# A quarter of the output projection's weights loaded early by GpSimd into partitions 64 to 127, in transfers of 8 rows

## The chip, the cores and the metric

One core of one Trainium2 chip. The metric is the time of one execution in device microseconds (us). The kernel before takes 192.46 us (median of 4 runs, 192.37 to 192.64).

## The reference

Grouped-query attention over a cache, with one projection before it and one after it; everything is bf16.

```python
q = (x @ wq).reshape(B, Sq, Hq, Dh).transpose(0, 2, 1, 3)        # B 8, Sq 4, D 512, Hq 32, Dh 128
k = jnp.repeat(k_cache, 4, axis=1); v = jnp.repeat(v_cache, 4, axis=1)   # 8 KV heads, Sk 2048
p = softmax(einsum("bhqd,bhkd->bhqk", q, k) * Dh ** -0.5)
o = einsum("bhqk,bhkd->bhqd", p, v)
out = o.transpose(0, 2, 1, 3).reshape(B, Sq, Hq * Dh) @ wo         # wo: 4096 x 512
```

The caches are 64 MB, wq and wo 4 MB each. All of it must be read once.

## The kernel before

The work is cut into 32 units (a pair of KV heads and a batch row). A unit loads 1 MB of K and 1 MB of V, each a 128-partition transfer of 8 KB rows, all from the Sync engine's queue, as buffers come free. TensorE (PE) transposes K, forms the scores, then the values and the sums of the softmax, in 64 half-unit steps. wo has four quarters of 1 MB. The parts that the change touches:

```python
loads = []
for u in range(NU + KA):                      # NU = 32, KA = 4
    if u < NU:
        loads.append(("k", u))
    if u >= KA - 1 and u - KA + 1 < NU:
        loads.append(("v", u - KA + 1))
    if u in (NU, NU + 1):                     # wo between the last three V
        loads.append(("wo", (u - NU, 0, WR if u == NU else 4)))
# ...
def to_wo_rows(p):                            # the heads' output, transposed to wo's row order
    perm = psum_l.tile([128, WR, T], BF16, tag="l", name="perm")
    for r in range(WR):                       # WR = 8
        nc.tensor.transpose(perm[:, r, :],
            nats[p][:, :, :].rearrange("t q r -> t r q")[:, r, :], ident[:T, :T])
    nc.vector.tensor_copy(out=oP[p][:, :, :], in_=perm[:, :, :])

def project(p, r0, n):                        # one quarter: 8 row groups x 2 column halves
    for half in range(2):
        for r in range(r0, r0 + n):
            nc.tensor.matmul(out_ps[half][:, :], lhsT=oP[p][:, r, :],
                rhs=wo_sb[:, p, r, half * DH : (half + 1) * DH],
                start=(p == 0 and r == 0), stop=(p == G2 - 1 and r == WR - 1))
# ...
        if step == NH - 1 - 2 * VB:           # all K and V issued: the rest of wo
            load_wo(1, 4, 4); load_wo(2, 0, WR); load_wo(3, 0, 4); load_wo(3, 4, 2); load_wo(3, 6, 2)
        if step == NH - 5:
            # out_ps allocated
            project(0, 0, WR)
        elif step == NH - 3:
            project(1, 0, 4)
# then: to_tokens(3), project(1, 4, 4), to_wo_rows(3), project(2, ..), project(3, ..), output
```

The softmax here doesn't subtract the row's maximum and nothing guards it: scores larger than these inputs give would overflow.

Of the kernel before, what the change touches and what calls it, by code (L numbers as in the profile page):

```python
# [8 lines left out]
BF16 = mybir.dt.bfloat16  # L9
# [5 lines left out]
def kernel(  # L15
# [9 lines left out]
    nc = tc.nc  # L25

    B, Sq, D = x.shape
# [4 lines left out]
    T = B * Sq  # L32
    R = D // 128
    G2 = Hkv // 2
# [3 lines left out]
    HP = 2 * rep  # L38
    scale = float(Dh) ** -0.5
    NU = G2 * B  # L40
    NH = 2 * NU
    KB = 7
    VB = 6
    L = 6
    KA = L // 2 + 1
    WR = HP
    DH = D // 2
# [5 lines left out]
    const = ctx.enter_context(tc.tile_pool(name="const", bufs=1))  # L53
    wpool = ctx.enter_context(tc.tile_pool(name="wpool", bufs=1))
    kpool = ctx.enter_context(tc.tile_pool(name="kpool", bufs=KB))
    vpool = ctx.enter_context(tc.tile_pool(name="vpool", bufs=VB))
# [5 lines left out]
    psum_l = ctx.enter_context(tc.tile_pool(name="psum_l", bufs=1, space=bass.MemoryType.PSUM))  # L62
# [12 lines left out]
    ident4 = const.tile([128, 128], FP32, name="ident4")  # L75
    oT_all = const.tile([128, Hq, B, Sq], BF16, name="oT_all")
    out_sb = [const.tile([T, DH], BF16, name=f"out_sb{i}") for i in range(2)]
    oP = [const.tile([128, WR, T], BF16, name=f"oP{p}") for p in range(G2)]
    ident = const.tile([128, 128], BF16, name="ident")
    ones = const.tile([128, 128], BF16, name="ones")  # L80
    probs = [const.tile([128, C, NQ], BF16, name=f"probs{i}") for i in range(L // 2 + 2)]
# [25 lines left out]
    def load_wo(p, r0, n):  # L107
        rows = wo[p * HP * 128 : (p + 1) * HP * 128, :].rearrange("(q r) j -> q r j", r=WR)
        nc.sync.dma_start(wo_sb[:, p, r0 : r0 + n, :], rows[:, r0 : r0 + n, :])
# [3 lines left out]
    loads = []  # L113
    for u in range(NU + KA):
        if u < NU:
            loads.append(("k", u))
        if u >= KA - 1 and u - KA + 1 < NU:
            loads.append(("v", u - KA + 1))
        if u in (NU, NU + 1):
            loads.append(("wo", (u - NU, 0, WR if u == NU else 4)))  # L120
    loads.reverse()

    def load_ready(nk, nv):

        while loads:
            kind, u = loads[-1]
            if kind == "wo":
                loads.pop()
                load_wo(*u)
                continue  # L130
            if u >= (nk + KB if kind == "k" else nv + VB):
                return
# [7 lines left out]
    for e in range(2):  # L140
        for g in range(2):
            nc.vector.tensor_copy(
                out=pick[:, e, g, :], in_=ident[:, :].rearrange("d (k e) -> d e k", e=2)[:, e, :]
# [12 lines left out]
    for p in range(G2):  # L156
        psq = psum_s.tile([128, HP, T], FP32, tag="s", name="psq")
        for h in range(HP):
            hh = p * HP + h
            for r in range(R):  # L160
                nc.tensor.matmul(  # L161
                    psq[:, h, :],
                    lhsT=wq_sb[:, r, hh * 128 : (hh + 1) * 128],
                    rhs=xT_sb[:, r, :],
                    start=(r == 0),
# [3 lines left out]
            out=qT_all[:, p, :, :, :],  # L169
            in_=psq[:, :, :].rearrange("d h (b s) -> d b h s", b=B),  # L170
            mul=scale,
        )
    for p in range(G2):
        pse = psum_s.tile([128, 2, B, NQ], FP32, tag="s", name="pse")
        for e in range(2):
            nc.tensor.matmul(  # L176
                pse[:, e, :, :],
                lhsT=pick[:, e, :, :],
                rhs=qT_all[:, p, :, :, :].rearrange("d b h s -> d (b h s)"),
                start=True,  # L180
                stop=True,
            )
        for g in range(2):
            rows = slice(g * 64, (g + 1) * 64)
            (nc.scalar.copy if g else nc.vector.tensor_copy)(  # L185
                out=q_bd[rows, p, :, :, g, :], in_=pse[rows, :, :, :]
            )

    wo_sb = wpool.tile([128, G2, WR, D], BF16, tag="w", name="wo_sb")
    kt = {}  # L190

    def transpose_part(i, part):
        u, hf = divmod(i, 2)
        c0 = hf * HC + part * (HC // 2)
        kp = psum_k.tile([128, HC // 4, 128], FP32, tag="k", name="kp")
        k4 = ks[u][:, :, :].rearrange("s c d -> s (c d)").bitcast(FP32)
        for j in range(HC // 4):
            w = (c0 // 2 + j) * 128
            nc.tensor.transpose(kp[:, j, :], k4[:, w : w + 128], ident4[:, :])  # L199
        kp2 = kp[:, :, :].rearrange("k j s -> k (j s)").bitcast(BF16)  # L200
        k_t = ktpool.tile([128, HC // 4, 128, 2], BF16, tag="kt", name="kt")
        kt2 = k_t[:, :, :, :].rearrange("k j s e -> k (j s e)")
        if part == 1 and hf == 1:
            nc.scalar.copy(out=kt2, in_=kp2)  # L204
        else:
            nc.vector.tensor_copy(out=kt2, in_=kp2)  # L206
        kt[(i, part)] = k_t

    def scores(i):
        u, hf = divmod(i, 2)  # L210
        p, b = units[u]
        pr = probs[u % len(probs)]
        s_ps = psum_s.tile([128, HC, NQ], FP32, tag="s", name="s_ps")
        for j in range(HC // 2):
            k_t = kt[(i, j // (HC // 4))]
            for e in range(2):
                nc.tensor.matmul(  # L217
                    s_ps[:, 2 * j : 2 * j + 2, :],
                    lhsT=k_t[:, j % (HC // 4), :, e],
                    rhs=q_bd[:, p, e, b, :, :],  # L220
                    start=(e == 0),
                    stop=(e == 1),
                )
        for g in range(2):
            rows = slice(g * 64, (g + 1) * 64)
            cols = slice(g * NQ // 2, (g + 1) * NQ // 2)
            nc.scalar.activation(  # L227
                out=pr[rows, hf * HC : (hf + 1) * HC, cols], in_=s_ps[rows, :, cols], func=EXP
            )
# [3 lines left out]
    def values(i):  # L233
        u, hf = divmod(i, 2)
        p, b = units[u]
        pr = probs[u % len(probs)]
        if hf == 0:
            o_ps[u] = psum_o.tile([128, NQ], FP32, tag="o", name="o_ps")
        for c in range(HC):
            cc = hf * HC + c  # L240
            nc.tensor.matmul(  # L241
                o_ps[u][:, :],
                lhsT=vs[u][:, cc, :],
                rhs=pr[:, cc, :],
                start=(cc == 0),
                stop=(cc == C - 1),
            )
# [3 lines left out]
    def norms(u):  # L251
        pr = probs[u % len(probs)]
        l_ps = psum_l.tile([128, LC, NQ], FP32, tag="l", name="l_ps")
        for c in range(0, C, LC):
            nc.tensor.matmul(  # L255
                l_ps[:, :, :],
                lhsT=ones[:, :],
                rhs=pr[:, c : c + LC, :],
                start=(c == 0),
                stop=(c + LC == C),  # L260
            )
        l_sb = small.tile([128, NQ], FP32, tag="l_sb", name="l_sb")
        nc.vector.tensor_reduce(  # L263
            out=l_sb[:, :], in_=l_ps[:, :, :].rearrange("d c q -> d q c"), axis=AX, op=ADD
        )
        r_sb = small.tile([128, NQ], FP32, tag="r_sb", name="r_sb")
        nc.vector.reciprocal(r_sb[:, :], l_sb[:, :])  # L267
        r_sbs[u] = r_sb
# [10 lines left out]
    nats = {}  # L279
# [14 lines left out]
        nats[p] = nat_sb  # L294

    def to_wo_rows(p):
        perm = psum_l.tile([128, WR, T], BF16, tag="l", name="perm")
        for r in range(WR):
            nc.tensor.transpose(
                perm[:, r, :],  # L300
                nats[p][:, :, :].rearrange("t q r -> t r q")[:, r, :],
                ident[:T, :T],
            )
        nc.vector.tensor_copy(out=oP[p][:, :, :], in_=perm[:, :, :])

    def project(p, r0, n):
        for half in range(2):
            for r in range(r0, r0 + n):
                nc.tensor.matmul(  # L309
                    out_ps[half][:, :],  # L310
                    lhsT=oP[p][:, r, :],
                    rhs=wo_sb[:, p, r, half * DH : (half + 1) * DH],
                    start=(p == 0 and r == 0),
                    stop=(p == G2 - 1 and r == WR - 1),
                )

    for step in range(-L - 1, NH):
        i, j = step + L + 1, step + L
        if i < NH:
            transpose_part(i, 0)  # L320
        if 0 <= j < NH:
            scores(j)
        if i < NH:
            transpose_part(i, 1)
        u, hf = divmod(step, 2)
        if step >= 0:
            p, b = units[u]
            if hf == 0:
                norms(u)
            values(step)  # L330
            if hf == 1:
                finish(u)
            elif p > 0 and b == 1:
                to_tokens(p - 1)
            elif p > 0 and b == 2:
                to_wo_rows(p - 1)
        load_ready(min((i + 1) // 2, NU), max((step + 1) // 2, 0))
        if step == NH - 1 - 2 * VB:
            assert not loads
            load_wo(1, 4, 4)  # L340
            load_wo(2, 0, WR)
            load_wo(3, 0, 4)
            load_wo(3, 4, 2)
            load_wo(3, 6, 2)
        if step == NH - 5:
            out_ps = [
                psum_s.tile([T, DH], FP32, tag="s", name=f"out_ps{n}") for n in range(2)
            ]
            project(0, 0, WR)
        elif step == NH - 3:  # L350
            project(1, 0, 4)

    to_tokens(3)
    project(1, 4, 4)
    to_wo_rows(3)
    project(2, 0, WR)
    project(3, 0, 4)
    project(3, 4, 2)
    project(3, 6, 2)
# [35 lines left out]
```

## Time and profile before

| what | before | where it is read |
|---|---|---|
| time | 192.46 us | median of the runs |
| span of the profiled execution | 191.0 us | page |
| DMA engines' time, main queue | 95.5% of the span | page, queues |
| PE busy | 81% | page |
| last K landed | 166.35 us | chain of waits |
| PE waits for data after that | 2.75 us | PE timeline |

A queue's share is the time of its packets over 16 engines' span.

### The profile page before, as it was taken

Reading aid. Unit: us, or ns where it says so; the run is one execution under the profiler, and the core shown is the slowest. Engines: PE = TensorE matmul, PEld = TensorE weight load, DVE = VectorE, ACT = ScalarE, POOL = GpSimd, SP = SyncE. Lnnn points to the kernel's source line nnn. Section 1 sums busy time; section 2 is a strip of 40 time slices with the busy share of each in tenths; the row PEclk is TensorE's granted clock in tenths of the full one; section 3 lists DMA queues with packets and bytes.
Section 4 is the critical chain, followed back from the end, with each engine's and each line's share of the span. In section 5 each row is a group of like instructions: output and inputs, shape, how many; then the busy total and the mean of one; then the engine's idle time right before and its main releaser. Section 6 shows DMA issues by size and latency. Waiting matters only on the chain.

```text
span 191.0 us, 6460 instructions
## 1 busy us (share of the span) xinstructions
PE 154.4 (81%) x2892; PEld 139.7 (73%) x2892; DVE 113.9 (60%) x220; ACT 86.2 (45%) x170; POOL 1.1 (1%) x8
## 2 busy tenths in 40 slices
PE   0019887899999999988888888988886899997783
PEld 0008776799999998877778888877775788885572
DVE  6401754577776777666666667766664677662420
ACT  2003466656566654555555444454554455551000
POOL 2000000000000000000000000000000000000000
PEclk9999999999999999999999999999999999999999
DMA  6999999999999999999999999999999999999940
GB/s 220 439 412 422 419 420 422 420 413 429 410 419 419 417 420 419 417 425 415 420 420 419 422 415 420 419 419 420 415 419 424 415 422 419 415 419 419 399 184 8
DMA packets 10539, 75.97 MB, mean 398 GB/s; under 512 B 1200, under 2 KB 1296, under 8 KB 1936
## 3 DMA queue, kind: packets, MB, share of 16 engines
q1 hardware_dynamic: 10464, 75.55, 95.5%
q8 instruction: 22, 0.36, 0.8%
q14 instruction: 5, 0.04, 0.1%
q10 hardware_dynamic: 48, 0.02, 0.0%
HBM read 75.53 MB, written 0.03 MB: 396 GB/s over the span
## 4 chain that ended last, share of the span: by engine, by line
DMA 90%; PE 7%; ACT 0%; DVE 0%; issue 0%; SPq 0%
DMA k_sb<-in_k_cache_dram 74%; DMA wo_sb<-in_wo_dram 9%; DMA x_sb<-in_x_dram 6%; PE psq L161 2%; PE out_ps L309 2%; PE kp L199 2%; PE pse L176 1%; DVE q_bd L185 0%; PE s_ps L217 0%; ACT q_bd L185 0%; PE xtp L152 0%; SPq L111 0%; ACT out_sb L362 0%; DVE xT_sb L155 0%
## 5 line engine op out<-in xcount | busy, mean ns | idle before, releaser
L199 PE MATMUL kp<-ident,k_sb 128*128 128x128 f32 x512 | 80.9, 284 | 10.6 <-DMA k_sb<-in_k_cache_dram 10.4
L206 DVE COPY kt<-kp 128x1024 bf16<-128x1024 bf16 x96 | 65.5, 685 | 26.6 <-PE kp L199 25.9
L227 ACT ACTIVATE probs<-s_ps 64x256 bf16<-64x256 f32 x128 | 48.3, 378 | 68.7 <-PE s_ps L217 67.9
L199 PEld LDWEIGHTS kp<-ident,k_sb 128*128 128x128 f32 x512 | 55.2, 143 | 12.0 <-issue 11.4
L217 PE MATMUL s_ps<-q_bd,kt 128*128 128x64 bf16 x1024 | 42.3, 193 | 3.1 <-ACT kt L204 2.6
L217 PEld LDWEIGHTS <-kt 128*128 128x128 bf16 x1024 | 39.7, 98 | 4.8 <-ACT kt L204 3.1
L241 PEld LDWEIGHTS <-v_sb 128*128 128x128 bf16 x1024 | 34.3, 96 | 9.4 <-DMA v_sb<-in_v_cache_dram 2.0
L263 DVE TENSOR_REDUCE l_sb<-l_ps 128x32 f32<-128x512 f32 x32 | 22.1, 692 | 24.5 <-PE l_ps L255 24.5
L241 PE MATMUL o_ps<-probs,v_sb 128*128 128x32 bf16 x1024 | 35.0, 176 | 1.0 <-DMA v_sb<-in_v_cache_dram 0.9
L204 ACT COPY kt<-kp 128x1024 bf16<-128x1024 bf16 x32 | 32.4, 1012 | 0.8
L255 PE MATMUL l_ps<-probs,ones 128*128 128x512 bf16 x64 | 19.1, 379 | 0.0
L267 DVE RECIPROCAL r_sb<-l_sb 128x32 f32<-128x32 f32 x32 | 11.3, 353 | 1.1
L152 PE MATMUL xtp<-ident,x_sb 32*128 32x32 bf16 x4 | 0.5, 189 | 13.7 <-DMA x_sb<-in_x_dram 13.5
L152 PEld LDWEIGHTS <-x_sb 32*128 32x128 bf16 x4 | 0.3, 112 | 13.8 <-DMA x_sb<-in_x_dram 13.5
L309 PE MATMUL out_ps<-wo_sb,oP 128*32 128x256 bf16 x64 | 7.6, 272 | 1.7 <-DMA wo_sb<-in_wo_dram 1.7
L168 ACT ACTIVATE qT_all<-psq 128x256 bf16<-128x256 f32 x4 | 1.5, 383 | 14.8 <-PE psq L161 14.8
L309 PEld LDWEIGHTS <-oP 128*32 128x32 bf16 x64 | 6.1, 96 | 2.5 <-issue 1.7
L362 ACT CAST out_sb<-out_ps 32x256 bf16<-32x256 f32 x1 | 0.4, 361 | 15.6 <-PE out_ps L309 15.6
L272 DVE TENSOR_TENSOR oT_all<-o_ps,r_sb 128x32 bf16<-128x32 f32 x32 | 5.8, 182 | 1.7 <-PE o_ps L241 1.5
L255 PEld LDWEIGHTS <-ones 128*128 128x128 bf16 x64 | 6.0, 98 | 0.8 <-issue 0.4
L185 DVE CAST q_bd<-pse 64x512 bf16<-64x512 f32 x4 | 2.6, 683 | 4.7 <-PE pse L176 4.7
L155 DVE COPY xT_sb<-xtp 128x32 bf16<-128x32 bf16 x4 | 0.5, 170 | 7.0 <-PE xtp L152 7.0
(23 smaller groups left out, 34.4 us busy)
## 6 DMA issues: line engine op xcount, KB each, us to landing
k_sb<-in_k_cache_dram SPq DMA_DIRECT2D x32, 1024.0 KB, 20.3
v_sb<-in_v_cache_dram SPq DMA_DIRECT2D x32, 1024.0 KB, 20.2
wq_sb<-in_wq_dram SPq DMA_DIRECT2D x1, 4096.0 KB, 12.5
wo_sb<-in_wo_dram SPq DMA_DIRECT2D x2, 1024.0 KB, 19.2
wo_sb<-in_wo_dram SPq DMA_DIRECT2D x3, 512.0 KB, 18.0
wo_sb<-in_wo_dram SPq DMA_DIRECT2D x2, 256.0 KB, 13.6
x_sb<-in_x_dram SPq DMA_DIRECT2D x1, 32.0 KB, 12.3
out_dram<-out_sb SPq DMA_DIRECT2D x1, 16.0 KB, 1.4
```

Source lines behind the costliest of these rows:

```text
L161: nc.tensor.matmul(psq[:, h, :], lhsT=wq_sb[:, r, hh * 128 : (hh + 1) * 128], rhs=xT_sb[:, r, :], start=(r == 0), stop=(r == R - 1),)
L199: nc.tensor.transpose(kp[:, j, :], k4[:, w : w + 128], ident4[:, :])
L204: nc.scalar.copy(out=kt2, in_=kp2)
L206: nc.vector.tensor_copy(out=kt2, in_=kp2)
L217: nc.tensor.matmul(s_ps[:, 2 * j : 2 * j + 2, :], lhsT=k_t[:, j % (HC // 4), :, e], rhs=q_bd[:, p, e, b, :, :], start=(e == 0), stop=(e == 1),
L227: nc.scalar.activation(out=pr[rows, hf * HC : (hf + 1) * HC, cols], in_=s_ps[rows, :, cols], func=EXP)
L241: nc.tensor.matmul(o_ps[u][:, :], lhsT=vs[u][:, cc, :], rhs=pr[:, cc, :], start=(cc == 0), stop=(cc == C - 1),)
L255: nc.tensor.matmul(l_ps[:, :, :], lhsT=ones[:, :], rhs=pr[:, c : c + LC, :], start=(c == 0), stop=(c + LC == C),)
L263: nc.vector.tensor_reduce(out=l_sb[:, :], in_=l_ps[:, :, :].rearrange("d c q -> d q c"), axis=AX, op=ADD)
L267: nc.vector.reciprocal(r_sb[:, :], l_sb[:, :])
L272: nc.vector.tensor_tensor(out=oT_all[:, p * HP : (p + 1) * HP, b, :], in0=o_ps[u][:, :].rearrange("d (h s) -> d h s", h=HP), in1=r_sbs[u][ ...
L309: nc.tensor.matmul(out_ps[half][:, :], lhsT=oP[p][:, r, :], rhs=wo_sb[:, p, r, half * DH : (half + 1) * DH], start=(p == 0 and r == 0), st ...
```

## The change

The intent, as the code shows it: one quarter of wo no longer comes through the queue that bounds the kernel. GpSimd loads it at the start into a tile of its own, in partitions 64 to 127, as eight transfers of 8 partitions, four apart. Each has a 4 KB transfer ahead of it that nobody reads. The quarter then has 64 partitions with 16 row groups in place of 128 with 8, so PE does 16 transposes and 32 matmuls for it, in place of 8 and 16.

```diff
+    HI = 2
-        if u in (NU, NU + 1):
-            loads.append(("wo", (u - NU, 0, WR if u == NU else 4)))
+        if u == NU:
+            loads.append(("wo", (0, 0, 4)))
+    wo_hi = const.tile([128, 2 * WR, D], BF16, name="wo_hi")
+    spare = const.tile([8, DH], BF16, name="spare")
+    wo2 = wo[2 * HP * 128 : 3 * HP * 128, :].rearrange("(q r) j -> q r j", r=2 * WR)
+    for base in (0, 32):
+        for m in range(4):
+            lo = base + m
+            nc.gpsimd.dma_start(spare[:, :], x.flatten_outer_dims()[:8, :DH])
+            nc.gpsimd.dma_start(
+                wo_hi[64 + lo : 64 + lo + 29 : 4, :, :], wo2[lo : lo + 29 : 4, :, :]
+            )
 ...
+        lo, nr = (64, 2 * WR) if p == HI else (0, WR)
+        for r in range(nr):
+            nc.tensor.transpose(perm[lo:, r, :], nat_r[:, r, :], ident[:T, :T])
 ...
+                    lhsT=oP[p][64:, r, :] if p == HI else oP[p][:, r, :],
+                    rhs=wo_hi[64:, r, cols] if p == HI else wo_sb[:, p, r, cols],
 ...
-            project(0, 0, WR)
+            project(HI, 0, 2 * WR)
         elif step == NH - 3:
-            project(1, 0, 4)
+            project(0, 0, 4)
```

(The renumbering of the later quarters follows from it.)

More of the change, by code (lines that the diff above doesn't have):

```diff
@@ L77 @@
     out_sb = [const.tile([T, DH], BF16, name=f"out_sb{i}") for i in range(2)]
-    oP = [const.tile([128, WR, T], BF16, name=f"oP{p}") for p in range(G2)]
+    oP = [const.tile([128, WR * (1 + (p == HI)), T], BF16, name=f"oP{p}") for p in range(G2)]
     ident = const.tile([128, 128], BF16, name="ident")
@@ L296, in to_wo_rows @@
     def to_wo_rows(p):
-        perm = psum_l.tile([128, WR, T], BF16, tag="l", name="perm")
-        for r in range(WR):
-            nc.tensor.transpose(
-                perm[:, r, :],
-                nats[p][:, :, :].rearrange("t q r -> t r q")[:, r, :],
-                ident[:T, :T],
-            )
-        nc.vector.tensor_copy(out=oP[p][:, :, :], in_=perm[:, :, :])
+        lo, nr = (64, 2 * WR) if p == HI else (0, WR)
+        perm = psum_l.tile([128, nr, T], BF16, tag="l", name="perm")
+        nat_r = nats[p][:, :, :].rearrange("t q r -> t (q r)").rearrange("t (q r) -> t r q", r=nr)
+        for r in range(nr):
+            nc.tensor.transpose(perm[lo:, r, :], nat_r[:, r, :], ident[:T, :T])
+        nc.vector.tensor_copy(out=oP[p][lo:, :nr, :], in_=perm[lo:, :, :])
     def project(p, r0, n):
         for half in range(2):
+            cols = slice(half * DH, (half + 1) * DH)
             for r in range(r0, r0 + n):
@@ L310, in project @@
                     out_ps[half][:, :],
-                    lhsT=oP[p][:, r, :],
-                    rhs=wo_sb[:, p, r, half * DH : (half + 1) * DH],
-                    start=(p == 0 and r == 0),
+                    lhsT=oP[p][64:, r, :] if p == HI else oP[p][:, r, :],
+                    rhs=wo_hi[64:, r, cols] if p == HI else wo_sb[:, p, r, cols],
+                    start=(p == HI and r == 0),
                     stop=(p == G2 - 1 and r == WR - 1),
@@ L339 @@
             assert not loads
-            load_wo(1, 4, 4)
-            load_wo(2, 0, WR)
+            load_wo(0, 4, 4)
+            load_wo(1, 0, WR)
             load_wo(3, 0, 4)
@@ L348 @@
             ]
-            project(0, 0, WR)
+            project(HI, 0, 2 * WR)
         elif step == NH - 3:
-            project(1, 0, 4)
+            project(0, 0, 4)
     to_tokens(3)
-    project(1, 4, 4)
+    project(0, 4, 4)
     to_wo_rows(3)
-    project(2, 0, WR)
+    project(1, 0, WR)
     project(3, 0, 4)
```

## The prediction

> **What bounds the kernel now.** I read the page's slices and queues first.
>
> ```profile
> span 191.0 us, 6460 instructions
> ...
> PE   0019887899999999988888888988886899997783
> ...
> DMA  6999999999999999999999999999999999999940
> ...
> q1 hardware_dynamic: 10464, 75.55, 95.5%
> q8 instruction: 22, 0.36, 0.8%
> q14 instruction: 5, 0.04, 0.1%
> ```
>
> The DMA row is 9 in all slices but the first and the last two: the 16 DMA engines never rest between 2 and 182 us, and PE has gaps. So the 75.55 MB of the main queue set the pace. The other two queues look negligible; they are not, as shown below.
>
> The chain that ended last says the same, and then the PE timeline of the tail shows where DMA hands over to PE:
>
> ```profile
> 146.53 19.83 DMA k_sb<-in_k_cache_dram
> 166.35 0.02 issue
> 166.37 17.98 DMA wo_sb<-in_wo_dram
> 184.35 0.04 issue
> 184.39 3.67 PE out_ps L309 x32
> ```
>
> ```profile
> 166.49 0.63 PE L199 MATMUL kp<-ident,k_sb 128*128 128x128 f32 x4 [0.37 <-DMA k_sb<-in_k_cache_dram]
> ...
> 172.37 0.95 PE L241 MATMUL o_ps<-probs,v_sb 128*128 128x32 bf16 x32
> 174.43 1.91 PE L309 MATMUL out_ps<-wo_sb,oP 128*32 128x256 bf16 x16 [1.10 <-DMA wo_sb<-in_wo_dram]
> 176.26 0.60 PE L255 MATMUL l_ps<-probs,ones 128*128 128x512 bf16 x2
> 176.95 0.96 PE L241 MATMUL o_ps<-probs,v_sb 128*128 128x32 bf16 x32
> 178.19 1.03 PE L309 MATMUL out_ps<-wo_sb,oP 128*32 128x256 bf16 x8 [0.28 <-DMA wo_sb<-in_wo_dram]
> 179.15 0.60 PE L255 MATMUL l_ps<-probs,ones 128*128 128x512 bf16 x2
> 180.69 0.96 PE L241 MATMUL o_ps<-probs,v_sb 128*128 128x32 bf16 x32 [0.94 <-DMA v_sb<-in_v_cache_dram]
> 181.94 0.62 PE L284 MATMUL nat<-ident,oT_all 128*32 128x128 bf16 x8 [0.28 <-DVE oT_all L272]
> ...
> 184.39 3.65 PE L309 MATMUL out_ps<-wo_sb,oP 128*32 128x256 bf16 x32 [0.34 <-DMA wo_sb<-in_wo_dram]
> ```
>
> From the landing of the last K (166.35) on, PE waits for data only 1.10, 0.09 (before 176.95), 0.28, 0.94 and 0.34 us: 2.75 us of 21.7. The tail is PE work as much as it is DMA.
>
> The trace also has, for each transfer, the times of the 16 increments of its semaphore[...]. Sorted, as lag behind the first of them, in us:
>
> ```
> landing of      first   lags of the 16
> 3rd K            20.15  0 to 0.31 for 15 of them, 0.63
> last K          161.57  .00 .01 .02 .17 .32 .58 .81 2.02 | 3.03 3.18 3.32 3.46 3.83 4.64 4.74 4.78
> last V          175.21  .00 .02 .04 .18 .35 .60 1.56 2.10 | 3.08 3.25 3.52 4.72 4.82 4.83 4.93 5.44
> last wo         181.57  .00 .01 .02 .14 .26 .56 1.46 1.98 | 2.99 3.15 4.58 4.68 4.72 4.81 4.96 5.30
> ```
>
> All engines start together; by the end eight are 3 to 5.3 us behind. Following the rows, a lag jumps by about 1.5 us, one engine at a time, at each of the 22 packets of q8; these hit the same eight engines in rounds, six of them three times and two twice (6x3 + 2x2 = 22). The other eight are almost untouched. A load has landed only when its slowest engine has.
>
> **The intent**, as I read it: give 1 MB to the eight engines that run ahead, through another queue, and take it out of the stream that all 16 share.
>
> [...]
>
> **The change part by part.**
> 1. Removed from the main queue: 1 MB of wo, 64 KB per engine. In the steady stream an 8 KB packet starts every 306 ns on an engine (309 ns each, overlapping by 3), so 8 x 0.306 = 2.45 us per engine. But this 1 MB lay after the last K, in the wo loads around and behind the last Vs. Half of it now leaves the queue before V of unit 30, the rest after the last V. Nothing ahead of the last K gets shorter.
> 2. Added: eight transfers of 8 rows of 16 KB. Each of their eight engines gets 8 x 16 KB = 16 packets' worth: 16 x 0.306 = 4.9 us, plus switching between queues. The five 8 KB packets of q14 raised an engine's lag by 0.39 to 0.52 where the bytes alone are 0.31, so I add some 0.1 per row: about 5.6 us. This comes within the first 30 us or so, ahead of every V and most K.
> 3. Added: eight loads of 512 B per row [...]. x may land some 2 or 3 us later than 13.43, and so PE starts later; PE regains that in the middle, where it waits for K anyway (10.4 us in 13 waits), and loads are issued some 20 us ahead, so the stream doesn't dry up.
> 4. PE: the quarter has 64 partitions, so 16 row groups and 32 matmuls where 16 were, and 8 more transposes around 146 us (hidden by waits). In the tail the 16 took 1.83 us (174.43 to 176.26), 0.114 each; 32 take 3.65. The 1.10 us wait before them goes.
>
> Now the tail. If the eight untouched engines get the load, the slowest of them at the last K has 0.8 to 2.0 (say 1.4) + 5.6 = 7.0 us of lag, against 4.78: the last K lands 2.2 us later. From there PE has: 6.0 us to values (172.37 - 166.35), giving 174.6; values 0.95; the 32 matmuls 3.65; norms 0.6; values 0.96; 8 matmuls 0.97; norms 0.6; values 0.96; 0.3 to the tokens. Sum 9.0: 183.5, against 181.94. The data is there in time: V of unit 30 at about 166.53 + 1.24 + 2.48 + 7.0 = 177.3 (wanted at 179.8), the last V at 179.7 (wanted at 182.3), the next quarter of wo at 176.53 + 7.0 = 183.5 (wanted near 185.6). So all waits of the tail vanish, PE sets the end, and the end moves by 183.5 - 181.9 = +1.6 us. 192.47 + 1.6 = about 194.1.
>
> **Rivals.**
> - *Balanced as intended:* drain time alone. The slow eight end at 5.30 - 2.45 = 2.85, the fast ones at 1.98 + 4.9 - 2.45 = 4.43, so the last landing is 0.9 us sooner. For it: the finish times above. Against it: the last K cannot come sooner, and PE from there on is nearly unbroken work. Even with the last K where it was, all waits gone (2.75) less 1.83 of added matmuls is under 1 us: 191.6 at best. A switching cost of nothing and a lag of 0.8 would give about 193.
> - *The wrong half:* the large transfers fall on the eight fetching engines [...]. Then the last K lands 5 to 5.6 us later, PE ends 4.5 to 5 later: about 197.2. [...]
> - *Spread over all 16:* 2.5 to 3 us on every engine, nearly the same shift at the last K as in the main case: 194.5.
> - *GpSimd held up:* [...] The loads then spread over more of the first 60 us; they are needed at 173, so the time stays as in the case that holds.
>
> **Range and chances.** Main case 60%, 193.0 to 195.3; intended balance with little cost 14%, 191.6 to 193; spread evenly 11%; wrong half 15%, 196 to 198. The 80% range is 192.2 to 196.8. Over 2% faster is below 188.6, which the PE tail forbids; over 2% slower is above 196.3, which needs the wrong half or far dearer switching.
>
> **What would show it.** A GpSimd queue with about 1 MB in the first 30 us. Landing lags of eight engines up by 5 to 6 us there, the other eight unmoved; a maximum of 6.5 to 7.5 at the last K, which lands near 168.5. In the tail: 32 matmuls of wo_hi in 3.65 us without a wait, and hardly a wait for V or wo behind them. Wrong if lags of more than 9 show (wrong half), if each row costs an engine well over 0.8 us, if PE's late start is never regained, or if the last K does not land later.

The forecast's sum came to 183.5 - 181.9 = +1.6 us, so 192.47 + 1.6 = about 194.1 us. The prediction reads the 16 increments of a load as one for each of the 16 DMA engines. The trace names no engine, so this is a reading; what the trace shows is that the last K's last increment came at 161.57 + 4.78 = 166.35 and that PE took that K up at 166.49. Of the 8448 records of 8 KB packets, 309 ns is the most frequent (3131) and 312 the median.

## More of the kernel before

A share near 100% tells that the engines are occupied; it does not tell how many bytes they move while they are. For that one needs the GB/s beside it. The view by stretches gives both, for 10 to 50 us and 50 to 90 us (columns: stretch, its length, busy time of PE, PE's weight loads, VectorE, ScalarE and GpSimd with counts, the clock that PE was granted as a share of full clock, DMA share, GB/s):

```profile
10.00:50.00 40.00, 32.67 (x583) 29.43 (x584) 20.87 (x39) 20.36 (x41) 0.00 (x0) 1.00 1.00 414
50.00:90.00 40.00, 38.27 (x754) 35.42 (x751) 29.05 (x57) 22.79 (x46) 0.00 (x0) 1.00 1.01 418
```

Here share and rate go together: 1.00 with 414, 1.01 with 418 GB/s.

## The result, and the profile after

The changed kernel takes 203.31 us (median of 4 runs, 202.85 to 205.35), the kernel before 192.46. The ratio is 1.058 (95% interval 1.051 to 1.066). A ratio is the mean time of one kernel's fast runs over that of the other's in the same rounds, so it is not quite the ratio of the medians. The predicted range ended at 196.8.

From the page of the changed kernel, the lines that answer to those of before:

```profile
span 201.3 us, 6528 instructions
...
PE   0006887899868788999888889788888899999983
...
PEclk9999999999999999999999999999999999799999
DMA  6989999999999999999999999999999999999500
GB/s 234 411 313 413 356 361 374 361 367 374 410 420 422 410 418 427 417 415 423 418 422 420 418 417 427 414 418 417 418 423 418 415 420 422 414 420 398 235 20 7
...
q1 hardware_dynamic: 10320, 74.50, 91.6%
q0 software_dynamic: 512, 1.08, 2.0%
q8 instruction: 23, 0.38, 0.8%
```

Look at the DMA row and the row below it together. Between the first slice and the last three the share is 8 or 9, nearly as before, but from the third to the tenth slice (10 to 50 us) the rate is 313 to 374 GB/s, but for one slice of 413; in the rest it is near 420. The same stretches as before, of the changed kernel:

```profile
10.00:50.00 40.00, 29.69 (x528) 26.71 (x528) 18.88 (x35) 18.62 (x38) 6.56 (x13) 1.00 1.00 366
50.00:90.00 40.00, 33.31 (x650) 30.54 (x647) 25.68 (x49) 19.79 (x39) 0.00 (x0) 1.00 1.01 416
```

At 10 to 50 us the engines are fully occupied (1.00) and move 366 GB/s in place of 414. That is 40 us x 48 GB/s = 1.9 MB less, or about 4.6 us of the stream, averaged over all 16 engines. The 1 MB that GpSimd loads is part of the 366, so it is not what is missing.

When it happens, the GpSimd timeline tells (a part of it):

```profile
15.51 0.52 POOL L199 DMA_DIRECT2D spare<-in_x_dram  x1 [5.12 <-DMA spare<-in_x_dram]
16.02 0.52 POOL L200 DMA_DIRECT2D wo_hi<-in_wo_dram  x1
20.62 0.52 POOL L199 DMA_DIRECT2D spare<-in_x_dram  x1 [4.08 <-DMA spare<-in_x_dram]
...
44.91 0.52 POOL L200 DMA_DIRECT2D wo_hi<-in_wo_dram  x1
```

Each small transfer waits for the one before it to land, because they share a tile, so the pairs come 5.1 to 7.6 us apart; the last large transfer is issued at 44.91 and has landed at 50.97. The slow stretch is just the time of these transfers.

The trace's packet records, counted in half microseconds around one pair, show what an engine does meanwhile ("busy" is the sum over all 16 engines; packets of 8 KB are those of K and V; a normal one takes 312 ns):

```
from us   8 KB packets started   of these over 450 ns   busy: main queue   busy: GpSimd queue
24.0               24                     0                   15.0               0.2
24.5               25                     1                   15.2               0.7
25.0               11                     4                   10.8               5.4
25.5               11                    11                    8.7               7.5
26.0               11                    11                   14.7               1.5
26.5               21                     0                   16.1               0.2
27.0               25                     0                   16.2               0.0
```

At 25.5 to 26.0 the eight 16 KB rows keep 7.5 engines busy, as good as eight. The other eight are busy with K and V as ever, but each of their packets takes about 600 ns, and 11 start where 25 did. So engines that carry nothing of the GpSimd transfer run at half speed. At 26.0 most of the rows have ended, and the packets that follow them on their own engines are slow too: a row's record (883 ns in the median of all 64) does not show all that it costs its engine.

At the end the chain of waits hands over from DMA to PE for good:

```profile
140.56 19.86 DMA k_sb<-in_k_cache_dram
160.43 0.14 issue
160.56 0.63 PE kp L212 x4
161.19 0.47 PE s_ps L230 x16
```

The K that lands at 160.43 is that of unit 28. By the landing records the same transfer landed at 151.47 before: 8.96 us of the loss are there by then. From 160.43 on the chain has PE and the engines that feed it, and no DMA. The PE timeline of the tail:

```profile
183.61 0.95 PE L254 MATMUL o_ps<-probs,v_sb 128*128 128x32 bf16 x32
184.49 3.66 PE L321 MATMUL out_ps<-wo_hi,oP 64*32 64x256 bf16 x32
188.09 0.60 PE L268 MATMUL l_ps<-probs,ones 128*128 128x512 bf16 x2
...
192.47 0.62 PE L297 MATMUL nat<-ident,oT_all 128*32 128x128 bf16 x8 [0.68 <-DVE oT_all L285]
...
194.48 3.67 PE L321 MATMUL out_ps<-wo_sb,oP 128*32 128x256 bf16 x32
```

All waits for V and wo that stood in the tail before are gone. The end of the matmuls is at 194.48 + 3.67 = 198.15, against 184.39 + 3.65 = 188.04 before: 10.1 later, of which 9.0 come from DMA before 160.43 and 1.1 from PE after it.

### The profile page after: what moved, and what is told of

It reads as the page before. It is cut to its first block, busy times and chain, and to the rows that moved or that the text cites. A ratio compares the mean times of both kernels' runs of the same rounds, so it can differ in the third digit from the quotient of the medians.

```text
span 201.3 us, 6528 instructions
## 1 busy us (share of the span) xinstructions
PE 158.7 (79%) x2916; PEld 143.6 (71%) x2916; DVE 114.7 (57%) x220; ACT 86.2 (43%) x170; POOL 9.4 (5%) x24
## 3 DMA queue, kind: packets, MB, share of 16 engines
q0 software_dynamic: 512, 1.08, 2.0%
## 4 chain that ended last, share of the span: by engine, by line
DMA 70%; PE 22%; ACT 3%; DVE 2%; issue 1%; SPq 0%; DVEq 0%
DMA k_sb<-in_k_cache_dram 62%; DMA x_sb<-in_x_dram 8%; PE kp L212 6%; PE out_ps L321 4%; PE s_ps L230 3%; PE o_ps L254 2%; PE psq L162 2%; ACT kt L217 2%; PE l_ps L268 1%; PE perm L314 1%; DVE l_sb L276 1%; PE pse L177 1%; ACT probs L240 1%; DVE kt L219 1%; PE nat L297 1%
## 5 line engine op out<-in xcount | busy, mean ns | idle before, releaser
L212 PE MATMUL kp<-ident,k_sb 128*128 128x128 f32 x512 | 81.9, 286 | 15.8 <-DMA k_sb<-in_k_cache_dram 15.8
L212 PEld LDWEIGHTS kp<-ident,k_sb 128*128 128x128 f32 x512 | 55.9, 144 | 17.7 <-issue 16.1
L321 PEld LDWEIGHTS <-oP 128*32 128x32 bf16 (+1 forms) x80 | 7.3, 95 | 1.1
L199 POOL DMA_DIRECT2D spare<-in_x_dram x8 | 4.3, 534 | 35.3 <-DMA spare<-in_x_dram 35.3
L321 PE MATMUL out_ps<-wo_sb,oP 128*32 128x256 bf16 x48 | 5.8, 273 | 0.0
```

Of the source, the lines that this page charges most:

```text
L199: nc.gpsimd.dma_start(spare[:, :], x.flatten_outer_dims()[:8, :DH])
L212: nc.tensor.transpose(kp[:, j, :], k4[:, w : w + 128], ident4[:, :])
L321: nc.tensor.matmul(out_ps[half][:, :], lhsT=oP[p][64:, r, :] if p == HI else oP[p][:, r, :], rhs=wo_hi[64:, r, cols] if p == HI else wo_sb ...
```

## The experiments

All had the kernel before beside them on the same chip, with medians of 192.48 to 192.57. The changed kernel itself ran with the first result above.

| run | median us | ratio to before (95% interval) | V of unit 5 landed: first engine, ninth behind it, last | K of unit 28 landed | 8 KB packets over 450 ns, first 60 us |
|---|---|---|---|---|---|
| before | 192.46 | | 49.91, 0.25, 51.74 | 151.47 | 6 |
| changed | 203.31 | 1.058 (1.051 to 1.066) | 55.60, 4.78, 61.72 | 160.43 | 197 |
| one more small transfer | 203.08 | 1.055 (1.053 to 1.057) | 55.02, 5.81, 63.10 | 162.21 | 259 |
| partitions 0 to 63 | 196.87 | 1.022 (1.020 to 1.025) | 50.31, 4.90, 56.57 | 155.37 | 6 |
| DMA part alone | 203.25 | 1.057 (1.052 to 1.062) | 55.75, 4.61, 62.34 | 162.23 | 198 |
| small transfers alone | 192.89 | 1.001 (1.000 to 1.003) | 50.16, 0.40, 52.06 | 151.74 | 7 |
| no small transfers | 203.65 | 1.060 (1.054 to 1.065) | 54.81, 4.74, 60.71 | 159.67 | 144 |
| PE part alone (wrong output) | 194.49 | 1.008 (1.004 to 1.013) | 49.79, 0.46, 51.83 | 151.66 | 7 |
| one transfer of 128 rows | 192.66 | 1.001 (0.999 to 1.002) | 52.42, 0.31, 54.19 | 154.09 | 6 |
| four transfers of 16 rows | 198.10 | 1.031 (1.026 to 1.035) | 55.32, 0.36, 57.17 | 156.96 | 23 |
| 0 to 63, no small | 199.17 (fast runs 196.36, 197.89) | 1.024 (1.020 to 1.028) | 50.13, 4.77, 56.77 | 156.60 | 6 |
| one transfer, matmuls early | 192.56 | 1.000 (0.999 to 1.001) | 52.42, 0.27, 54.52 | 154.06 | 6 |

The landing columns are the increments of the load's semaphore (the counter that signals its landing) for the same load in each profile, 16 of them, sorted, and read as one for each engine. "Ninth behind it" separates two halves of eight engines, where there are two. With one more small transfer, the last large transfer was issued at 52.35 only, so that row's V column lacks part of it. The last column cannot be compared between runs with and without the small transfers: without them the rows had started by 23 us (four transfers of 16 rows: by 17), partly beside the 32 KB rows of wq, which it does not count.

The two theories at the start: (A) the 8-row transfers run on eight engines but write the half of the partitions that the other eight write with K and V ("crossing"), and the two streams then slow each other; (B) GpSimd transfers as such, or their reads of HBM (where the caches and weights lie), slow every engine. No record shows which engine writes which partitions, so A is a supposition that the runs test.

### 1. One more small transfer ahead of the others

```diff
+    nc.gpsimd.dma_start(spare[:, :], x.flatten_outer_dims()[8:16, :DH])
     for base in (0, 32):
         for m in range(4):
...
+    nc.gpsimd.dma_start(spare[:, :], x.flatten_outer_dims()[16:24, :DH])
```

> The changed kernel with one more small GpSimd transfer ahead of the first (and one after the last, so that their number stays even): [...] the large transfers fall on the other eight engines. Theory A ([...] both halves are then slowed, an 8 KB packet of the main queue takes 600 ns in place of 312 and a 16 KB row 880 ns in place of 611): [...] the 600 ns packets of the main queue disappear, a row takes 611 to 650 ns, one half of the engines loses nothing but the small transfers, and the last-K wait of PE comes 3 to 5 us sooner than 160.4; time 196 to 200 us. Theory B (GpSimd transfers cost every engine the same, whatever half they use[...]): slow packets stay at about 600 ns, time 202 to 206 us.

203.08 us, slow packets as before. Theory A as I had put it, with large transfers that one more small one moves to the other eight engines, missed. Either B holds or the transfers cannot be steered this way. By itself this run does not tell which.

### 2. The same transfers into partitions 0 to 63

```diff
-                wo_hi[64 + lo : 64 + lo + 29 : 4, :, :], wo2[lo : lo + 29 : 4, :, :]
+                wo_hi[lo : lo + 29 : 4, :, :], wo2[lo : lo + 29 : 4, :, :]
```

(and the same half for the transposes and matmuls that use it)

> The changed kernel with the quarter of wo in partitions 0 to 63 in place of 64 to 127; same transfers, same order, same rows of HBM, same matmul shapes. Theory A [...]: [...] the 600 ns packets disappear [...], time 196 to 200 us. Theory B [...]: nothing changes, 202 to 206 us with slow packets of 600 ns.

196.87 us. The same rows of HBM, the same number, size and order of transfers; only the destination's half differs, and 6.4 us are gone. The stretches of this run:

```profile
10.00:50.00 40.00, 31.00 (x587) 28.09 (x592) 20.84 (x40) 20.73 (x41) 6.62 (x13) 1.00 1.01 415
50.00:90.00 40.00, 34.28 (x668) 31.90 (x673) 26.70 (x51) 20.25 (x41) 0.00 (x0) 1.00 1.01 418
```

The rate at 10 to 50 us is 415 GB/s again. In the packet records the 600 ns packets are gone (6 over 450 ns, as before the change) and a 16 KB row takes 619 ns (median) in place of 883. B falls: the GpSimd queue moved 1.08 MB in 512 packets in both, from the same rows of HBM. Eight engines lose 0.40 us (50.31 - 49.91), the other eight 4.9 more, which is 8 rows x 0.61.

The landings also tell that the rows run on the same eight engines in both kernels. No record names an engine, but the instruction fetches (the packets of q8, at each of which one engine's lag jumps by about 1.5 us) mark them. At the K of unit 28 the eight less delayed engines have lags of 0, 0.56 and then 2.47 to 4.42 us in the changed kernel, and of 0, 0.03 and then 2.96 to 4.80 here: two engines that fetches hardly touched and six that they hit. Runs 1 and 5 show the same pattern (0, 0.16, 2.66 to 4.80 and 0, 0.51, 3.37 to 4.80). So the engines stayed, and what changed is the half that they write.

### 3. The DMA part alone

The kernel before with the 16 GpSimd transfers added; nobody reads their tile, and all of wo still comes through the main queue.

```diff
+    # wo_hi, spare and the loop of 16 GpSimd transfers, word for word as in the change
     kt = {}
```

> The kernel before with the 16 GpSimd transfers of the change added, into a tile that nobody reads: all of wo still comes through the main queue, and PE does what it did before (16 matmuls, 8 transposes). Correct output. Theory A with my reading that 9 of the 10.8 us come from the DMA engines and about 2 from PE (16 transposes in 1.97 us, a stretch of half clock): the stalls between 6 and 50 us are the same, the last landings come 8 to 10 us later than before, the full clock is granted all the time, time 200 to 203 us. If the loss were on PE, the time would be 193 to 196 us.

203.25 us with PE's work unchanged. The loss is in the transfers. Time and landing lie just above the expected ranges (the K of unit 28 comes 10.8 us later than before). As this kernel moves 1 MB more than the changed one, at its end (the last V lands at 190.75, against 186.54), the equal times do not say that PE's part costs nothing. The expectation of full clock all the time was wrong: the profile has half clock for 3.4 us twice, at 55.2 and 92.8, which shows that such stretches are not a matter of the added PE work.

### 4. The small transfers alone

```diff
+            nc.gpsimd.dma_start(spare[:, :], x.flatten_outer_dims()[:8, :DH])   # eight times, no large ones
```

(Cut: the tiles and the loop around it, as in the change.)

> The kernel before with only the eight small GpSimd transfers of 4 KB added. Theory A: they cost [...] at most 1.2 us per engine: 192.5 to 194 us. Rival: a fixed cost of each GpSimd transfer on all 16 engines of 0.3 to 0.4 us [...], which would make the loss of 5.8 us that even the fastest engine showed: eight transfers would then cost some 2.5 to 3 us, 195 to 195.5 us.

192.89 us; the first engine is 0.25 us later at V of unit 5, after eight transfers. So these cost 0.03 us each there, and not a fixed 0.3 us.

### 5. The large transfers alone

```diff
-            nc.gpsimd.dma_start(spare[:, :], x.flatten_outer_dims()[:8, :DH])
```

> The changed kernel without the eight small transfers; the eight large ones stay. Theory A1 (a GpSimd transfer of 8 rows always runs on the same eight engines[...], whatever came before it[...]): [...] slow packets of 600 ns on one half, eight engines lose about 8 x 1.22 = 9.8 us and the others 8 x 0.61 = 4.9; time 202 to 204 us. Theory A2 [...]: four of eight cross and four match, every engine loses 4.9 us, time 197 to 199 us.

203.65 us, with one half of the engines 4.9 us later and the other 9.6 (54.81 + 4.74 - 49.91). Had the transfers alternated between the two sets of eight engines, all engines would have lost the same. So, as the pattern under run 2 shows too, with an additional small transfer, with one ahead of each, or with none, the 8-row GpSimd transfers ran on the same eight engines. The small transfers steered nothing.

### 6. The PE part alone

```diff
-        if u == NU:
-            loads.append(("wo", (0, 0, 4)))
+        if u in (NU, NU + 1):
+            loads.append(("wo", (HI, 0, WR) if u == NU else (0, 0, 4)))
...
-                    rhs=wo_hi[64:, r, cols] if p == HI else wo_sb[:, p, r, cols],
+                    rhs=wo_sb[64:, HI, r % WR, cols] if p == HI else wo_sb[:, p, r, cols],
```

> Wrong output on purpose: the changed kernel's PE work (16 transposes and 32 matmuls of 64 rows for one quarter) on the loads of the kernel before, in their old order and without any GpSimd transfer; the quarter's second 64-row half is read from the wrong place. The DMA loss is gone, so this is the price of the PE part alone. Theory: 1.83 us of added matmuls less the waits in the tail that they fill (1.1 before them and parts of the later ones), and 1.3 us more of transposes around 150 us that PE's waits hide: 192.5 to 194 us. Rival: the longer transposes push PE behind for good, 195 us or more.

194.49 us, above the expected 192.5 to 194. The four runs fall in two groups: 192.80 where the mean granted clock was 1.000, and 194.28 to 194.75 where it was 0.972 to 0.991. In the profiled one (194.28) a stretch of half clock of 3.4 us began at 163.5, in the part of the run where PE no longer waits for data. So the 64-partition form costs 0.3 us by itself, by the one run at full clock, and 1.7 to 2.2 in the runs with less. That the clock makes the difference is read from these four runs and not tested by itself. The kernel before has such stretches too (granted clock 0.982 to 1.000 in its runs) and is not slower for them.

### 7. One transfer of 128 rows

```diff
+    wo_q = const.tile([128, WR, D], BF16, name="wo_q")
+    nc.gpsimd.dma_start(wo_q[:, :, :], wo[: HP * 128, :].rearrange("(q r) j -> q r j", r=WR))
```

(the kernel before otherwise, with this quarter out of the main queue)

> The kernel before with its first quarter of wo loaded early by one GpSimd transfer of 128 partitions into a tile of its own[...]; PE does what it did before. Theory: no slow packets, every engine is 2.5 us later (64 KB, 8 x 0.306) until the last K, the last K lands 2.5 us later than 166.35, the waits of the tail (2.75 us) take most of it up: 192 to 194 us. If the cost were in GpSimd transfers as such, 196 us or more.

192.66 us: the same as before. Every engine is 2.5 us later at V of unit 5, and the K of unit 28 lands 2.6 us later (154.09), without slow packets. The tail gives it back, as its waits are gone:

```profile
175.08 0.95 PE L245 MATMUL o_ps<-probs,v_sb 128*128 128x32 bf16 x32
175.96 1.92 PE L313 MATMUL out_ps<-wo_q,oP 128*32 128x256 bf16 x16
177.81 0.60 PE L259 MATMUL l_ps<-probs,ones 128*128 128x512 bf16 x2
...
184.22 3.67 PE L313 MATMUL out_ps<-wo_sb,oP 128*32 128x256 bf16 x32
```

### 8. Four transfers of 16 rows

```diff
-    for base in (0, 32):
-        for m in range(4):
-            lo = base + m
-            # (cut: the small transfer, then the one of 8 rows)
+    for lo in range(4):
+        nc.gpsimd.dma_start(
+            wo_hi[64 + lo : 64 + lo + 61 : 4, :, :], wo2[lo : lo + 61 : 4, :, :]
+        )
```

> The changed kernel with four GpSimd transfers of 16 rows (partitions 64 to 127 in steps of 4) in place of eight of 8, and no small ones. Theory A1: each of the 16 engines gets one row of each; [...] every row takes about 1.2 us and every engine loses 4 x 1.22 = 4.9 us; no engine loses 9.8. Last K about 5 us later than before, time 197 to 199 us. If the crossing did not matter, 4 x 0.61 = 2.45 us per engine and 194 to 195 us.

198.10 us. All 16 engines are 5.4 us later (55.32 - 49.91), with no split into halves (0.36 to the ninth). Each has only four rows, 4 x 0.61 = 2.45 us if nothing collided; 4 x 1.22 = 4.9 is what theory A gives if the rows are slowed to half rate, all 64 going to partitions 64 to 127 (estimate). This is the number that theory A gave and that no theory of GpSimd overhead gives, as there are half as many transfers.

### 9. Both faults mended

Run 2 without the small transfers.

```diff
-            nc.gpsimd.dma_start(spare[:, :], x.flatten_outer_dims()[:8, :DH])
```

> The change as it would stand with both faults mended that the runs showed: partitions 0 to 63, no small transfers. Theory: [...] rows take 611 to 626 ns, eight engines lose 8 x 0.61 = 4.9 us and the others next to nothing; the small transfers cost 0.3 us at most, so 196.3 to 197 us, still 2% slower than before, as two of the loaded engines are also among those that fetch instructions. Rival (the small transfers still did something useful): slower than the 196.87 of the run with them.

The runs took 196.36, 197.89, 200.46 and 200.73 us with granted clocks of 1.000, 0.988, 0.983 and 0.983; the last two count as slow, and so does the profile. The fast runs are 1.024 times the time of before. Whether the small transfers cost anything here, these four runs do not settle; they do not make up for anything either. The change in its mended form stays slower.

### 10. An attempt at a version faster than both

```diff
-            project(0, 0, WR)
+            # two matmuls that add the stored bf16 sum of the first quarter (identity x part_sb)
...
+            elif p == 2 and b == 4:
+                project_first()      # the 16 matmuls of the first quarter, into part_sb, near 100 us
```

(The loads are those of run 7.)

> An attempt to beat both: the run with one early 128-partition transfer, with the first quarter's 16 matmuls moved from the tail to about 100 us, where PE waits for K, and their bf16 sum added back by 2 matmuls. If the tail is bound by PE alone, 14 x 0.114 = 1.6 us less: 191.1 us. If it is bound by DMA as well (the last V lands near 180.2 and the following wo near 184.1, against 180.56 and 184.22 at which PE uses them), 0.1 to 0.4 us less: 192.3 to 192.6 us. I expect the second.

192.56 us, no gain. In run 7 the data of the tail comes just in time: by the landing records the last V is there at 180.21, and PE takes it up at 180.56. With fourteen matmuls less, PE waits instead: in this run's trace 0.92 us for the V of unit 30, 0.27 for the last V and 0.18 for wo. The tail is bound by DMA and PE at once, so I found nothing that beats the kernel before.

## Why the prediction was wrong

**The step that failed is part 2 of the change**, "about 5.6 us" on the eight engines that carry the rows, with "the other eight unmoved". Against before, the fastest engine of the unloaded half lost 5.7 us by V of unit 5 (55.60 - 49.91), and the loaded half some 4.8 more, 10.5. The size of a row on an engine by itself was right: in run 2, with the rows in the other partitions, the loaded half lost 5.3 and the other 0.4. What the sum lacked was the destination. With it the last K landed 9.0 us later (175.32 against 166.35), where the prediction had 2.2.

What the runs put in its place is a simple account. On the same eight engines, rows for partitions 0 to 63 slowed these eight alone, and rows for partitions 64 to 127 slowed the other eight as well: 197 of the 8 KB packets of the first 60 us took over 450 ns (579 in their median, against 312 of all), and a 16 KB row 883 in place of 619. The estimates below suppose that in the second case two streams share something, both at half rate. With 0.61 us for an undisturbed row (two packets of 0.306; run 2 measured 0.619), a 16 KB row then costs its engine 2 x 0.61 = 1.22 us, and one of the other eight engines loses half of that time:

| | loaded engines | others |
|---|---|---|
| 8 rows to partitions 0 to 63 (estimate) | 8 x 0.61 = 4.9 | 0 |
| measured, partitions 0 to 63 | 5.3 | 0.4 |
| 8 rows to partitions 64 to 127 (estimate) | 8 x 1.22 = 9.8 | 8 x 0.61 = 4.9 |
| measured, changed kernel | 10.5 | 5.7 |
| measured, no small transfers | 9.6 | 4.9 |
| 4 rows on all 16, to partitions 64 to 127 (estimate) | 4 x 1.22 = 4.9 | |
| measured, 16 rows | 5.4 | |

That the destination half decides it, for transfers that stay on the same engines, is shown by run 2 against the changed kernel; runs 7 and 8 agree. What the two streams share was not shown: no record names a place or an engine. The half rate is the author's estimate, which fits these numbers. A row's own record is 883 ns and not 1220; the packet records put the rest into the slow packets behind it. Added up over all engines until 60 us, the rows take 57 us and the main queue's packets 68 us more than before, 125 of the 130 us that the 16 increments of V of unit 5 are late in sum. The 0.5 us by which 16 rows exceed the estimate have no explanation.

**Two premises behind that step fell too.**
- That the small transfers place the large ones. Runs 1 and 5 show that the 8-row transfers used the same eight engines whatever came before them. I had named this possibility under the wrong-half rival, but had priced it at 197.2 without the collision. Run 2 (196.9), where the collision is absent, comes near that figure by another path, so the agreement is in part chance: its last K lands 3.9 us later (170.25 against 166.35), not 5 to 5.6.
- That the eight engines untouched by instruction fetches are one half, so that the last K would land 2.2 us later. Run 2, without the collision, has 3.9. It tells the halves apart by their load. At 112.4 us its lags were 0, 0.06, 1.48, 1.59, 2.98, 3.22, 3.39, 3.43 for the unloaded eight and 4.81, 4.86, 4.96, 5.32, 6.20, 6.29, 6.47, 6.66 for the loaded. At 50.3 they had been 0 to 1.97 and 4.90 to 6.26. Six of the unloaded had by then been hit by fetches, so the untouched engines are in both halves, mostly in the loaded one. Neither half could have taken the load freely.

**What held.** x landed 3.0 us later (16.40 against 13.43), PE's late start was regained, the 32 matmuls took 3.66 us without a wait, and all waits of the tail for data vanished, so that PE set the end. The prediction put the most that could be gained at under 1 us, because the removed megabyte lay behind the last K. That fits run 7, where the same megabyte, loaded early without a collision, changed the time by 0.1 us. With the measured 8.96 us at the K of unit 28 and the measured 1.1 of PE behind it, the same chain gives 192.5 + 10.1 = 202.6, near the 203.3 of the result. (One slip in part 1 cost nothing: all of the removed 1 MB stood ahead of the last V, not half of it, and the sum for the last V has it so.)

**The PE term.** The 1.1 us consist of 16 more matmuls, eight more transposes and half clock for 3.4 us from 173.1 on, less the waits that were there before. The 16 transposes of the 64-partition form take longer than twice the eight:

```profile
170.31 1.97 PE L314 MATMUL perm<-ident,nat_sb 32*64 32x32 bf16 x16 [0.39 <-DVE l_sb L276]
```

Before, eight took 0.61 (at 161.35). Run 6 prices the whole PE part at 0.3 to 2.2 us, by the clock. The stretch at 173.1 lasted 3.41 us with a granted share of 0.50, while PE had been working since 160.6 with gaps of 0.4 at most. What sets such stretches off stays open. All four runs of the changed kernel had some (clock 0.975 to 0.992), and the slowest, 205.35, had the lowest clock.

## What to carry to other kernels

Before you move a load to partitions of one half, try both halves: here transfers of eight rows to partitions 64 to 127 slowed the eight engines that carried them and the eight that did not (203.31 us), to partitions 0 to 63 the first eight alone (196.87). The profile's busy share did not tell (1.00 in both kernels), only the GB/s beside it (366 against 414). The same megabyte as one transfer over all 128 partitions cost the stream no more than its bytes, 2.5 us per engine. When a stream is the bound, look for the last transfer that the end hangs on: bytes taken from behind it and put in front of it did not pay here, even without a collision.
